# A gated linear recurrence and a squared-ReLU block: first two units by pairs of heads, loads ordered behind x, weights landing in other buffers

## The chip, the cores and the metric

The kernel runs on one core of one Trainium2 chip. The metric is the device time of one execution in microseconds (us). A core has five engines that work at the same time and wait for each other through semaphores: PE (TensorE, matrix products and transposes into PSUM banks), DVE (VectorE, element-wise work), ACT (ScalarE, functions and copies), POOL (GpSimd, here almost only as an issuer of DMAs) and SP (SyncE, an issuer of DMAs). Each engine carries out its own list of instructions strictly in order: one that has to wait holds up all that stand behind it in the list.

## The reference

```python
# (B, H, S, D) = (4, 8, 768, 48); all float32
mag = sqrt(a_re**2 + a_im**2)
scale = minimum(mag, 0.999) / (mag + 1e-06)
a = (a_re + i a_im) * scale                     # a complex gate for each channel
for t in range(S):
    S_re, S_im = a[t] * (S_re + i S_im) + k[t] v[t]^T    # a D x D state per head
    y[t] = q[t] @ S_re
x = y as (3072 tokens, 384)
out = (maximum(x @ w_in, 0) ** 2) @ w_out       # w_in 384 x 2048, w_out 2048 x 384
```

The two weight matrices come in as 64-bit floats and are turned into 32-bit floats on the chip; everything else is 32-bit.

## The kernel before, in words

**Units.** `fast_path` cuts the 3072 tokens into six units of 512. A sequence has 768 tokens, so the second unit (number 1) and the fifth (number 4) hold the end of one sequence and the start of the next ("cross"). Each unit passes through four stages, `load`, `chain`, `pairs` and `dense`; eight heads are held as two halves z = 0, 1 of four heads, and handled as four pairs i = 0..3, two pairs to a half.

**Chain (L822 to L1138), mostly DVE and ACT.** For each half, `roots` (L831: squares, logarithm, exponential, a Newton step) and `normalise` (L852) bring the gates to their scaled form; `inner` (L868) multiplies them up over four neighbouring tokens; `inverse` (L887) forms reciprocals. The totals are transposed on PE (`turned`, L934), run through a scan over the unit (`scan`, L1024, and `scan_x`, L976), and transposed back (L1085). Then `apply` (L1106) makes the scaled queries Q~ and keys K~ of one half: eleven DVE instructions on 128x768 elements (L1117, L1121 four times, L1124, L1126, L1132 four times, keys first), written into the work buffer `ff[z]`. After the two key products `gather` (L1149) copies K~ into the buffer `KC[z]` by DMAs of 32 partitions each, sixteen for each half (twelve where the unit is "cross" or ends a sequence). For units 0 and 1 (`EARLY = 2`) SP issues them, for the others POOL.

**Pairs (L1171).** For each pair of heads Q~ and K~ are transposed into a buffer `QT`: in units 0 and 1 by PE (`turn_pe`, L1202, four steps of four transposes each, ACT copies each out of PSUM), in the others by DVE and twelve DMAs of 64 KB on SP for each pair (`turn`, L1181). Then `score` (L1223) forms the 128x128 products with the mask on DVE, `keep` (L1240) the states K~^T v and their sums, and `mix` (L1271) the output y, which ACT copies to `yts` and SP spreads by two or three DMAs into `xT`, the transposed input of the dense block. `turn_pe` of unit 1 and `keep` take turns on the two PSUM banks `tr0` and `tr1`; `turn_pe` of unit 0 uses the dense banks d0 to d2.

**Dense (L1311), two groups of 256 tokens in a unit.** In a group, eight blocks of two column tiles of W_in (L1326: six products of 128x256 in a block, each shown as two matmuls) go through ReLU and square on ACT (L1333, L1334); then two accumulations over all W_out (L1344), an ACT copy (L1348), and four output DMAs on POOL (L1353).

**Weights.** Each matrix comes in eight pieces of 768 KB (`fetch`, L737, on POOL), and `convert` (L743) makes 32-bit floats of each with one ACT and three DVE instructions (L750, L753, L755, L759). Raw data need a buffer: `raw1` and `raw2` (L713, L719) name it for each piece. Four W_in pieces land in what later holds W_out, three in the g buffers of the dense block, one in the v buffer of unit 1; W_out pieces 0 to 3 take the last two slots of W_out's own buffer in turn, 4, 6 and 7 the three QT buffers, 5 the v buffer of unit 1. A buffer can only be fetched into once what was in it has been used. At the end `inspect` (L761) reads all sixteen pieces once more into the work buffers `ff`, where DVE looks at exponents (L774, L776); `verdict` (L1356) waits for it and for other sums.

**The order.** Nothing is issued as it is written. Every instruction or small group is a step of `Plan` (L481) with an engine, an estimated duration, keys that it reads and writes, and a rank. `order` (L515) runs a list schedule on those estimates: whenever an engine is free it takes the ready step with the lowest rank. The resulting order is emitted, and on the chip each engine keeps to it, with real waits for data and buffers only. So an estimate or a key has two effects: it moves a step in the list of its engine, and it holds nothing at run time. Ranks: pairs (1, n), W_in conversions (2, 0.3), W_out conversions (2, 0.6), chain (2, n), dense and weight fetches (3, ...), inspection (5, i).

Of the kernel before, what the change touches and what calls it, by code (L numbers as in the profile page):

```python
# [576 lines left out]
def fast_path(ctx, tc, q, k, v, a_re, a_im, moe_w_in, moe_w_out, out, flag):  # L577
# [6 lines left out]
    C = 128  # L584
# [53 lines left out]
    xT = sb("xT", NM * 4 * G).rearrange("p (m t) -> p m t", m=NM)  # L638
# [71 lines left out]
    def w2slot(s):  # L710
        return w2u[:, s * 2 * PW:(s + 1) * 2 * PW], [("w2", 2 * s), ("w2", 2 * s + 1)]

    raw1 = ([w2slot(s) for s in (3, 2, 1, 0)]  # L713
# [4 lines left out]
            + [(vv[1].bitcast(U32), [("v", 1)])])  # L718
# [4 lines left out]
            (QT[1].bitcast(U32)[:, 0:2 * PW], [("QT", 1)])]  # L723

# [12 lines left out]
    def fetch(i):  # L737
        src, t, keys, _, n, _ = piece(i)
        dma(pool, [("gate",)], keys,
            lambda: pool.dma_start(out=t.rearrange("p (m f) -> p m f", m=n), in_=src),  # L740
            (CONV, i), 2 * PW * 4 * C, 4.0)

    def convert(i):  # L743
        _, t, keys, dst, n, wk = piece(i)
        t3 = t.rearrange("p (m f two) -> p m f two", m=n, two=2)
# [15 lines left out]
    def inspect(i):  # L761
# [6 lines left out]
        dma(pool, [], keys,  # L768
# [53 lines left out]
    def chain(n):  # L822
# [7 lines left out]

        def roots(z):  # L831
# [3 lines left out]
                accum_out=sums[:, n, z:z + 1]), rank)  # L835
            step("DVE", tt(Y), key(z, 0, 1), key(z, 2), lambda: dve.tensor_tensor(
                out=m2, in0=f0, in1=f1, op=ALU.add), rank)
            step("ACT", ac(Y), key(z, 2), key(z, 0), lambda: act.activation(
                out=f0, in_=m2, func=AF.Ln), rank)
            step("ACT", ac(Y), key(z, 0), key(z, 1), lambda: act.activation(  # L840
                out=f1, in_=f0, func=AF.Exp, scale=-0.5), rank)
            step("ACT", ac(Y), key(z, 1), key(z, 3), lambda: act.activation(
                out=t, in_=f1, func=AF.Square), rank)
# [6 lines left out]
            step("DVE", 2 * tt(Y), key(z, 1, 2, 3), key(z, 3), newton, rank)  # L850

        def normalise(z):  # L852
            f0, f1, _, t = col[z]
            step("ACT", ac(Y), key(z, 3), key(z, 0), lambda: act.activation(
                out=f0, in_=t, func=AF.Copy, scale=0.999), rank)
            step("ACT", ac(Y), key(z, 3), key(z, 1), lambda: act.activation(
                out=f1, in_=t, func=AF.Copy, scale=-1e-6, bias=1.0), rank)
            step("DVE", tt(Y), key(z, 0, 1), key(z, 0), lambda: dve.scalar_tensor_tensor(
                out=f0, in0=f0, scalar=1.0, in1=f1, op0=ALU.min, op1=ALU.mult), rank)
# [3 lines left out]
                op=ALU.mult), rank)  # L863
            step("ACT", ac(Y), key(z, 3), [], lambda: act.activation(
                out=junk[:, 0:Y], in_=t, func=AF.Square, saturate=False,
                accum_out=sums[:, n, 2 + z:3 + z]), rank)
# [133 lines left out]
        def product(dst, xx, y, size, reads, writes):  # L1000
# [16 lines left out]
            step("DVE", 3 * tt(cnt), reads, writes + key(0, 0, 1), go, rank)  # L1017
# [6 lines left out]
        def scan():  # L1024
# [22 lines left out]
            for s in (1, 2, 4):  # L1047
                if s < span:
                    product(tv[:, 0:2, :, s:span], tv[:, 0:2, :, s:span],
                            lambda lo, hi, s=s: tv[:, lo:hi, :, 0:span - s], 40, I, I)  # L1050
                    step("DVE", 0.12, I, I, lambda s=s: minus(top, s, span, tv), rank)
# [54 lines left out]
        def apply(z):  # L1106
            a = A[z].rearrange("p (r h c d) -> p r h c d", r=2, h=HH, c=W)
            qk = QK[z].rearrange("p (r h c d) -> p r h c d", r=2, h=HH, c=W)
            xh = xn.rearrange("p r (h d) -> p r h d", h=H)[:, :, ts(z, HH)]
# [3 lines left out]
            def over(j):  # L1113
                return xh[:, j].unsqueeze(2).to_broadcast([C, HH, W, D])
# [13 lines left out]
            for j in (1, 0):  # L1128
# [6 lines left out]
                if j:  # L1135
                    gather(n, z)
# [322 lines left out]
```

## Time and profile before

| what | us |
|---|---|
| median of three runs (lowest, highest) | 773.3 (770.9, 773.61) |
| the profiled execution | 769.64 |
| its span, first to last instruction | 767.9 |
| PE busy, of the span | 661.5 |
| DVE busy | 506.2 |
| first matmul of the dense block | 106.88 |
| end of the last matmul of the dense block | 756.3 |

The profiled execution took 1.7 us more than its span, and 3.7 us less than the median of the runs. Of a PE row the profile counts two matmuls for each 32-bit product. A "stage" below is a stretch between two times from the start of the span. In the rows of the timeline the first two numbers are start and busy time of a run of equal instructions, and what stands in brackets is the idle time of the engine ahead of it and what ended that. In rows of stages, the numbers behind the stretch are its length, then for each engine the busy time and the number of instructions, then the granted clock of TensorE as a share of full speed (PEclk), the busy share of the DMA engines and their rate.

### The profile page before, as it was taken

How to read it: one execution, taken by the hardware profiler on the slowest of the kernel's cores; microseconds unless marked ns; L12 is line 12 of the kernel's file. 1: busy time of each engine (PE TensorE's matmuls, PEld its weight loads, DVE VectorE, ACT ScalarE, POOL GpSimd, SP SyncE). 2: the span in 40 equal slices, each digit the busy share in tenths (PEclk: the TensorE clock that was granted, in tenths of full speed). 3: DMA queues.
4: the chain of work that ended last, by engine and by line, in shares of the span. 5: the costliest groups of instructions: out<-in, count | busy, mean ns of one | idle time of the engine just before them, and what ended most of it. 6: DMA issues, size and time to landing. Idle time of an engine off the chain costs nothing.

```text
span 767.9 us, 10212 instructions
## 1 busy us (share of the span) xinstructions
PE 661.5 (86%) x3566; PEld 506.5 (66%) x3566; DVE 506.2 (66%) x978; ACT 346.7 (45%) x589; POOL 181.1 (24%) x349
## 2 busy tenths in 40 slices
PE   0014948999998999999999999999999998999994
PEld 0013836777776769858688677588676796686862
DVE  4999987999476797286995287982678975610000
ACT  6762266565466622478322568122765221041320
POOL 5400033420005053051162330250110541311101
PEclk9999977999998999999999999999999999999997
DMA  9721595200713026550046840054600399800000
GB/s 304 229 83 38 151 260 128 42 21 24 194 51 62 2 62 162 149 134 11 11 116 153 170 88 2 23 150 107 185 12 0 83 266 316 292 11 10 11 5 21
DMA packets 55932, 79.43 MB, mean 103 GB/s; under 512 B 11200, under 2 KB 37568, under 8 KB 55872
## 3 DMA queue, kind: packets, MB, share of 16 engines
q1 hardware_dynamic: 40768, 38.95, 19.8%
q0 software_dynamic: 15104, 39.74, 18.5%
q8 instruction: 30, 0.49, 0.3%
q14 instruction: 30, 0.25, 0.1%
HBM read 48.76 MB, written 4.72 MB: 70 GB/s over the span
## 4 chain that ended last, share of the span: by engine, by line
PE 49%; DVE 16%; ACT 7%; DMA 6%; SPq 2%; issue 2%; POOL 0%; DVEq 0%; POOLq 0%; ACTq 0%
PE d L1326 19%; PE d L1344 19%; DMA QT<-aq 5%; PE sc L1233 4%; PE tr L1249 3%; DVE f L876 2%; SPq L1197 2%; DVE f L1012 2%; DVE f L1014 2%; PE yp L1279 2%; DVE e L1016 1%; PE yp L1283 1%; DVE f L1016 1%; PE tr L1216 1%; DVE x L986 1%
## 5 line engine op out<-in xcount | busy, mean ns | idle before, releaser
L1326 PE MATMUL d<-xT,w 128*128 128x256 f32 x1152 | 264.4, 387 | 13.8 <-DMA xT<-yt 13.8
L1344 PE MATMUL d<-w,g 128*128 128x384 f32 x768 | 255.3, 488 | 0.0
L1326 PEld LDWEIGHTS d<-xT,w 128*128 128x128 f32 x1152 | 220.2, 194 | 48.8 <-issue 14.5
L1344 PEld LDWEIGHTS d<-w,g 128*128 128x128 f32 x768 | 144.2, 191 | 94.0 <-issue 2.0
L1353 POOL DMA_DIRECT2D out_dram<-ot x96 | 47.3, 499 | 352.9 <-ACT ot L1348 352.7
L1333 ACT ACTIVATE g<-d 128x512 f32<-128x512 f32 x96 | 57.1, 594 | 127.7 <-PE d L1326 127.6
L818 POOL DMA_DIRECT2D v<-in_v_dram x96 | 55.6, 586 | 91.6 <-PE yp L1283 26.7
L1236 DVE TENSOR_TENSOR A<-sc,mask 128x512 f32<-128x512 f32 x48 | 32.0, 685 | 49.6 <-PE sc L1233 49.6
L1334 ACT ACTIVATE g<-g 128x512 f32<-128x512 f32 x96 | 60.6, 631 | 3.1
L1157 POOL DMA_DIRECT2D KC<-f x104 | 51.0, 497 | 37.0 <-DVE f L1132 18.6
L1233 PE MATMUL sc<-QT 96*128 96x128 f32 x384 | 50.9, 283 | 10.2 <-DMA QT<-aq 7.0
L1233 PEld LDWEIGHTS sc<-QT 96*128 96x128 f32 x384 | 47.6, 196 | 13.9 <-issue 8.2
L1371 DVE TENSOR_SCALAR flag<-tr 1x1 int32<-1x1 f32 x1 | 0.1, 147 | 81.8 <-PE tr L1370 81.8
L1348 ACT COPY ot<-d 128x384 f32<-128x384 f32 x24 | 11.5, 478 | 90.2 <-PE d L1344 80.4
L1121 DVE TENSOR_TENSOR f<-aq,xn 128x768 f32<-128x768 f32 x48 | 42.6, 949 | 1.8 <-ACT xn L1085 1.7
L1132 DVE TENSOR_TENSOR f<-aq 128x768 f32<-128x768 f32 x48 | 43.3, 952 | 0.4
L1289 ACT COPY yt<-yp 112x512 f32<-112x512 f32 x24 | 14.0, 583 | 62.6 <-PE yp L1283 60.4
L1279 PE MATMUL yp<-A,v 128*48 128x128 f32 x384 | 38.0, 283 | 1.6 <-DVE A L1236 1.6
L934 PE MATMUL tr<-perm,xn 128*128 128x128 f32 x36 | 6.1, 301 | 37.3 <-ACT xn L907 37.3
L876 DVE TENSOR_TENSOR f<-aq 128x384 f32<-128x384 f32 x72 | 36.9, 554 | 0.7
L1279 PEld LDWEIGHTS yp<-A,v 128*48 128x48 f32 x384 | 23.1, 125 | 10.6 <-issue 6.3
L934 PEld LDWEIGHTS tr<-perm,xn 128*128 128x128 f32 x36 | 4.7, 153 | 38.6 <-issue 28.8
(145 smaller groups left out, 806.0 us busy)
## 6 DMA issues: line engine op xcount, KB each, us to landing
QT<-aq SPq DMA_DIRECT2D x192, 64.0 KB, 2.4
f<-in_moe_w_in_dram POOLq DMA_DIRECT2D x8, 768.0 KB, 8.7
f<-in_moe_w_out_dram POOLq DMA_DIRECT2D x8, 768.0 KB, 6.9
KC<-f POOLq DMA_DIRECT2D x104, 48.0 KB, 2.1
v<-in_v_dram POOLq DMA_DIRECT2D x96, 48.0 KB, 2.8
out_dram<-ot POOLq DMA_DIRECT2D x96, 48.0 KB, 1.8
xT<-yt SPq DMA_DIRECT2D x36, 96.0 KB, 4.6
aq<-in_a_re_dram SPq DMA_DIRECT2D x8, 384.0 KB, 3.8
```

The source lines that it names most:

```text
L818: lambda i=i, c=c, src=src: pool.dma_start(out=t[32 * c:32 * c + 32, i], in_=src[c]), vrank, 32 * 1536, 4.0,
L876: dve.tensor_tensor(out=f, in0=a[:, :, :, c - 1], in1=a[:, j, :, c].unsqueeze(1).to_broadcast([C, 2, HH, D]), op=ALU.mult)
L1121: lambda j=j, f=f, r=r: dve.tensor_tensor(out=f[:, r], in0=a[:, r], in1=over(j), op=ALU.mult), rank)
L1132: lambda j=j, r=r, o=o: dve.tensor_tensor(out=o[:, :, :, r * D:(r + 1) * D], in0=qk[:, j], in1=a[:, r], op=ALU.mult), rank)
L1157: lambda i=i, c=c: queue.dma_start(out=kc[32 * c:32 * c + 32, i], in_=nat[32 * i:32 * i + 32, c]),
L1233: pe.matmul(sa[:, j], lhsT=T[:, j, 1, h], rhs=T[:, j, 0, h], start=True, stop=True)
L1279: pe.matmul(ypair[64 * h:64 * h + D, ts(j, C)], lhsT=v5[:, j, 2 * i + h], rhs=aa[h][:, j], start=True, stop=at[j] is None)
L1326: pe.matmul(ps[:, j], lhsT=w1[:, f // FP, m, ts(f % FP, C)], rhs=xT[:, m, base:base + G], start=(m == 0), stop=(m == NM - 1))
L1333: act.activation(out=o, in_=ps, func=AF.Relu)
L1334: act.activation(out=o, in_=o, func=AF.Square)
L1344: pe.matmul(ps, lhsT=gt[:, f % 2, ts(i, C)], rhs=w2[:, f], start=(f == 0), stop=(f == NF - 1))
L1353: dma(pool, [("ot", o)], [], lambda c=c, o=o, dst=dst: pool.dma_start(out=dst[c], in_=ots[o][32 * c:32 * c + 32]), rank, 32 * DM * 4)
```

## The change

- **apply by pairs.** In units 0 and 1 `apply` runs once for each pair of heads (`np = 1`): the same eleven instructions on 384 instead of 768 elements, twice; `turn_pe` and `keep` of a pair wait for their own pair only. The copies of K~ go by pairs too (half as long, twice as many), in turn on POOL and SP. Units 2 to 5 keep the whole half and POOL.
- **Loads behind xT.** In the plan, q and k of unit 1, v of every later unit, five W_out pieces (1, 6, 7, then 2, 3) and the inspection depend on an xT being written (that of unit 0, of the unit two before, of unit 0, and of the last unit). W_out pieces 0, 4 and 5 are fetched ahead of the first `pairs`.
- **Buffers.** W_in piece 0 lands in `KC[1]` and piece 7 in the second half of `xT` (which becomes two blocks, one for even units and one for odd) instead of a W_out slot and the v buffer of unit 1.
- **Dense in two parts.** In the first group of each unit the first three blocks begin with the two row tiles m = 0, 1 of xT for their first column tile, and add m = 2 (the last two pairs of heads) afterwards.
- **Ranks and estimates.** `roots` and `normalise` of unit 1 get rank (2, 0.25), ahead of the weight conversions; the scan's products are estimated 0.24 us longer, `minus` at 0.18 for 0.12 us, the xT DMAs with 2.4 for 1.8 us of latency.

```diff
-    xT = sb("xT", NM * 4 * G).rearrange("p (m t) -> p m t", m=NM)
+    xT = sb("xT", 2 * NM * L).rearrange("p (n m t) -> p n m t", n=2, m=NM)
...
-    raw1 = ([w2slot(s) for s in (3, 2, 1, 0)]
+    raw1 = ([(KC[1].bitcast(U32), [("KC", 1, 0), ("KC", 1, 1)])]
+            + [w2slot(s) for s in (2, 1, 0)]
...
-            + [(vv[1].bitcast(U32), [("v", 1)])])
+            )
+    raw1 = [(three(t), keys) for t, keys in raw1]
+    raw1.append((xT[:, 1].bitcast(U32), [("xT", 1, m) for m in range(NM)]))
...
-    def fetch(i):
+    def fetch(i, early=True):
...
-        dma(pool, [("gate",)], keys,
+        dma(pool, [("gate",)] if early else [("xT", 0, NM - 1)], keys,
...
     def inspect(i):
...
-        dma(pool, [], keys,
+        dma(pool, [("xT", (NU - 1) % 2, NM - 1)], keys,
...
     def load(n):
...
-                        dma(queue, [], [(name, z)],
+                        dma(queue, [("xT", 0, NM - 1)] if n == 1 and half else [], [(name, z)],
...
-                dma(pool, [] if n else [("gate",)], [("v", n % 2)],
+                dma(pool, [("xT", n % 2, NM - 1)] if n else [("gate",)], [("v", n % 2)],
...
+        first = (CHAIN, 0.25) if n == 1 else rank
...
-            step("DVE", 3 * tt(cnt), reads, writes + key(0, 0, 1), go, rank)
+            step("DVE", 3 * tt(cnt) + 0.24, reads, writes + key(0, 0, 1), go, rank)
...
-        def apply(z):
+        def apply(z, p, np):
...
+            hs = ts(p, 2) if np == 1 else slice(0, HH)
+            a, qk = a[:, :, hs], qk[:, :, hs]
+            nh = 2 * np
+            n1 = Y * np // 2
...
+            own = ff[z][:, p * Z:(p + np) * Z]
...
-                    gather(n, z)
+                    gather(n, z, p, np)
         for z in range(2):
-            apply(z)
+            if n < EARLY:
+                apply(z, 0, 1)
+                apply(z, 1, 1)
+            else:
+                apply(z, 0, 2)
...
-    def gather(n, z):
+    def gather(n, z, p, np):
...
-                dma(queue, [("f", z, 2), ("f", z, 3)], [("KC", z)],
-                    lambda i=i, c=c: queue.dma_start(
+                queue = sp if n < EARLY and c % 2 else pool
+                dma(queue, keys, [("KC", z, q_) for q_ in range(p, p + np)],
+                    lambda i=i, c=c, queue=queue: queue.dma_start(
...
-                step("PE", 0.46, [("f", z, s4) for s4 in range(4)], [(b,)], go, rank)
+                step("PE", 0.46, [("f", z, 2 * (i % 2) + j) for j in range(2)], [(b,)],
+                     go, rank)
...
     def dense(n, grp):
...
+        split = 3 if grp == 0 else 0
+        for f2, b, ps, o, s in blocks[:split]:
+            f = 2 * f2
+            step("PE", 0.87, [("w1", f // FP)] + [("xT", n % 2, m) for m in range(NM - 1)],
+                 [(b,)], part_of(f, ps[:, 0], range(NM - 1)), rank)
+        for f2, b, ps, o, s in blocks:
             for j in range(2):
                 f = 2 * f2 + j
...
+                late = f2 < split and j == 0
+                step("PE", 0.43 if late else 1.3,
...
+                     part_of(f, ps[:, j], (NM - 1,) if late else range(NM)), rank)
...
             for i in range(NPIECE):
                 fetch(i)
+            for i in range(NPIECE):
+                convert(i)
         chain(n)
         if n == 0:
...
+            for j in (0, 4, 5):
+                fetch(NPIECE + j)
         pairs(n)
         if n == 0:
...
+            for j in (1, 6, 7):
+                fetch(NPIECE + j, False)
+            for j in (0, 1):
+                convert(NPIECE + j)
+            for j in (2, 3):
+                fetch(NPIECE + j, False)
+            for j in range(2, NPIECE):
+                convert(NPIECE + j)
```

More of the change, by code (lines that the diff above doesn't have):

```diff
@@ L723, in fast_path @@
             (QT[1].bitcast(U32)[:, 0:2 * PW], [("QT", 1)])]
+    raw2 = [(two(t), keys) for t, keys in raw2]
     def piece(i):
@@ L849, in newton @@
                                          op0=ALU.add, op1=ALU.mult)
-            step("DVE", 2 * tt(Y), key(z, 1, 2, 3), key(z, 3), newton, rank)
+            step("DVE", 2 * tt(Y), key(z, 1, 2, 3), key(z, 3), newton, first)
         def normalise(z):
@@ L1128, in apply @@
+            for r, op in ((0, ALU.subtract), (1, ALU.add)):
+                step("DVE", tt(n1), kf[0] + kf[1], [("a", z)],
+                     lambda r=r, op=op: dve.tensor_tensor(
+                         out=a[:, r], in0=f4[:, 0, r], in1=f4[:, 1, 1 - r], op=op), rank)
             for j in (1, 0):
-                o = ff[z][:, j * Z:(j + 1) * Z].rearrange("p (c h e) -> p h c e", c=W, h=HH)
+                o = own[:, j * nh * W * R:(j + 1) * nh * W * R].rearrange(
+                    "p (c h e) -> p h c e", c=W, h=nh)
```

120 lines of the change are left out of this document (54 added, 66 removed).

## The prediction

> **What bounds the kernel now.** I read the busy times by stage first, then PE's timeline from the first pair of heads to the second unit's dense block, then DVE's, SP's and POOL's in that stretch, and last PE's waits near the end.
>
> ```profile
> span 767.9 us, 10212 instructions
> 68.00:106.90 38.90, 33.19 (x305) 30.08 (x305) 36.72 (x59) 14.29 (x24) 4.19 (x7) 0.92 0.63 161
> 106.90:119.44 12.54, 2.16 (x6) 1.01 (x5) 9.13 (x12) 11.44 (x16) 6.29 (x12) 0.64 0.97 234
> 119.44:234.00 114.56, 112.90 (x626) 87.58 (x626) 89.99 (x174) 66.55 (x117) 19.78 (x37) 0.98 0.28 72
> 234.00:346.00 112.00, 107.78 (x576) 82.07 (x575) 77.60 (x150) 54.08 (x92) 36.59 (x69) 0.97 0.40 97
> 673.60:756.40 82.80, 82.80 (x323) 60.54 (x321) 0.96 (x4) 21.59 (x37) 7.88 (x16) 1.00 0.04 10
> 756.40:767.90 11.50, 0.05 (x2) 0.00 (x0) 0.15 (x1) 0.45 (x1) 1.96 (x4) 0.63 0.10 26
> ```
>
> From 119.44 on PE hardly rests: 112.90 of 114.56 us, then 107.78 of 112.00, and 82.80 of 82.80 in the last dense block. So the end is the time at which PE gets steady work, plus that work, plus the holes left in it, plus a tail of 11.5 us that the change doesn't touch. The holes are ahead: 10.4 us in 106.90 to 119.44, where the DMA engines are busy at 0.97.
>
> ```profile
> 68.03 5.36 PE L1216 MATMUL d<-ident,f 128*96 128x128 f32 x24 [10.15 <-DVE f L1132]
> 106.88 0.99 PE L1326 MATMUL d<-xT,w 128*128 128x256 f32 x2
> 116.64 1.19 PE L1326 MATMUL d<-xT,w 128*128 128x256 f32 x2 [8.77 <-DMA xT<-yt]
> 119.44 22.62 PE L1326 MATMUL d<-xT,w 128*128 128x256 f32 x92 [1.61 <-DMA xT<-yt]
> 187.12 1.04 PE L1216 MATMUL tr<-ident,f 128*96 128x128 f32 x8
> 195.81 1.14 PE L1249 MATMUL tr<-v,KC 128*96 128x48 f32 x12
> 231.56 0.43 PE L1279 MATMUL yp<-A,v 128*48 128x128 f32 x4
> 237.83 16.68 PE L1326 MATMUL d<-xT,w 128*128 128x256 f32 x62 [3.46 <-DMA xT<-yt]
> ```
>
> Of the rows from 106.88 to 119.44 the first holds the first matmuls of dense unit 0; the next stands 8.77 us until xT lands. But the hinge is the last row: dense unit 1 starts at 237.83, once its own xT is there, and everything behind it is PE work in a row. Between 119.44 and 237.83 PE does dense unit 0 and, from 187.12, pairs of unit 1; pairs start when unit 1's chain is through. An earlier start of dense unit 0 alone therefore buys nothing: PE would run out of it while the pairs of unit 1 go on. **The two bounds on dense unit 1** are PE's own work and unit 1's chain with its pairs. I work out both.
>
> **PE's bound.** The work between is 112.90 us; its cold part is 2.8 us: 92 matmuls took 22.62, 246 ns each, where 66 later take 14.41, 218 ns:
>
> ```profile
> 346.05 14.41 PE L1326 MATMUL d<-xT,w 128*128 128x256 f32 x66
> 66.32 10.15 SPq L1157 DMA_DIRECT2D KC<-f  x16
> 77.71 11.54 SPq L1157 DMA_DIRECT2D KC<-f  x16
> 280.07 6.01 POOL L1157 DMA_DIRECT2D KC<-f  x12 [3.39 <-DVE f L1132]
> KC<-f SPq DMA_DIRECT2D x56, 48.0 KB, 2.0
> xT<-yt SPq DMA_DIRECT2D x36, 96.0 KB, 4.6
> ```
>
> So 110 us after dense unit 0 begins to run freely. When is that? In unit 0 the copies of K~ keep SP from 66.32 to 89.25 (77.71 + 11.54), 0.63 us an issue. With as many on SP (32, of half the size) and as many more on POOL at 0.50 us (6.01 for 12), each batch of eight takes 5 us on SP behind its pair's keys, and the first pair turns about 4 us earlier than 68.03. The last pair's mix ended at 106.9; I estimate 100 (bounds 94, if only K~ held it, and 106.9, if ACT's and PE's lists hold it as before). Then ACT, the issue and the landing: 107 to 119.44 before, 12.5 us under 0.97 of DMA; with q, k, v and five weight pieces behind, about 5, the 4.6 us of the median row. Dense unit 0 starts near 105 (98 to 115; the upper end if POOL's loads still collide), and PE's bound for dense unit 1 is 215 (208 to 225).
>
> **The chain's bound, step by step from 237.83.**
>
> ```profile
> 140.67 1.02 DVE L876 TENSOR_TENSOR f<-aq 128x384 f32<-128x384 f32 x2
> 141.72 0.36 DVE L880 TENSOR_TENSOR aq<-f 128x192 f32<-128x192 f32 x1
> 110.93 0.96 DVE L846 SCALAR_TENSOR_TENSOR f<-f 128x768 f32<-128x768 f32 x1 [2.10 <-ACT f L842]
> 114.06 0.96 DVE L846 SCALAR_TENSOR_TENSOR f<-f 128x768 f32<-128x768 f32 x1 [1.18 <-DMA xT<-yt]
> 126.47 0.56 DVE L753 TENSOR_SCALAR w<-w 128x768 uint32<-128x768 uint32 x1 [3.02 <-DMA w<-in_moe_w_out_dram]
> 129.49 0.96 DVE L759 CUSTOM_DVE_ANT_0 w<-w 128x1536 uint16<-128x1536 uint16 x1 [1.46 <-ACT w L750]
> 176.87 4.43 DVE L1121 TENSOR_TENSOR f<-aq,xn 128x768 f32<-128x768 f32 x5 [0.84 <-ACT xn L1085]
> 183.20 3.57 DVE L1132 TENSOR_TENSOR f<-aq 128x768 f32<-128x768 f32 x4
> 185.19 7.48 SPq L1157 DMA_DIRECT2D KC<-f  x12
> ```
>
> DVE is the pacemaker here: unit 1's `inner` starts at 140.67, behind apply of unit 0 and all conversions, and the four waits above (2.10, 1.18, 3.02, 1.46) are 7.8 us of idle time.
> 1. Halving costs DVE: an instruction of 768 takes 0.89 us in a row (3.57 for 4), two of 384 take 1.05 (141.72 less 140.67), so 0.16 for each of 22 instructions in unit 0: +3.4.
> 2. Weights 0, 4 and 5 of W_out come early, and roots of unit 1 go first, so DVE has work in hand in those waits. Between none and all of 7.8 comes back; I take 5.9, nearer the upper end because the two longest waits are for weights. With step 1: −2.5 (−4.4 to +3.4) at `inner`. The re-ranked steps themselves add nothing, they change places. The early weights run before the first K~ is issued; if they slipped behind it they would cost the forecast one landing of K~, 2.0. W_in piece 0 in K~'s second buffer is converted first of all, long before 77.71, and q and k of unit 1, which leave SP's list ahead of xT, are only used behind `inner`: nothing for these.
> 3. Unit 1's first pair waits for 10 instructions of 0.525, 5.2 us, instead of 176.87 to 186.77, 9.9 (one of z = 1 lay in between): −4.6. The second halves are needed later and lie beside PE's work.
> 4. K~ of unit 1: twelve issues took 7.48 us on SP, so keep followed at 195.81, 8.7 behind the first turn. Six on POOL and six on SP take 3.7, and with 2.0 of landing K~ is there 2.9 sooner. The scores go ahead of keep on PE in any case, so 0 to −2.9; I take −2.2.
> 5. Dense in two parts: three blocks' first parts, 2.6 us of PE work by the plan's three times 0.87, which is the four matmuls of a part at 218 ns, run under the 3.46 us wait: 0 to −2.6; −2.6. In other units no such wait shows, and the split costs nothing, since it only reorders matmuls.
> 6. Four pairs took 44.4 us (187.12 to 231.56), with blocks of dense unit 0 between their steps. If that unit starts near 105, its work ends before the last two pairs, and these don't stand behind blocks: 2 us a pair, −4 (0 to −6).
>
> Sum −15.9: dense unit 1 at 222, 7 us behind PE's bound, so the chain decides and xT's faster landing in unit 0 is more than is needed. Unit 2's chain takes its buffers after unit 1's pairs, so it moves along.
>
> **Behind that.** The inspection's loads share the DMA engines with the last unit's transposes:
>
> ```profile
> 612.14 1.54 POOL L769 DMA_DIRECT2D f<-in_moe_w_in_dram  x2
> 666.08 1.46 POOL L769 DMA_DIRECT2D f<-in_moe_w_out_dram  x2
> QT<-aq SPq DMA_DIRECT2D x192, 64.0 KB, 2.4
> 631.36 6.53 DMA QT<-aq
> 649.84 0.49 PE L1233 MATMUL sc<-QT 96*128 96x128 f32 x2 [1.04 <-DMA QT<-aq]
> 653.01 1.91 PE L1233 MATMUL sc<-QT 96*128 96x128 f32 x10 [2.68 <-DMA QT<-aq]
> 486.20 0.55 PE L934 MATMUL tr<-ident,f 128*128 128x128 f32 x3 [1.33 <-ACT f L1080]
> ```
>
> A transpose's DMA takes 6.53 against a median of 2.4, and PE waits 1.04 + 2.68 = 3.7 us. Behind the last xT the inspection no longer meets them: −3.7. Its cover is the last dense block, 82.8 us, and it took 55 (612.14 to 667.54); DVE is idle there, so it costs nothing unless it takes over 80. The wait of 1.33 at L934 comes of a scan estimated too short; longer estimates put other products first: −1.0 (0 to −1.3). v behind xT moves little, its buffer was bound to the same pairs.
>
> All: 769.64 − 15.9 − 3.7 − 1.0 = 749.0 for a profiled execution. The median of the runs lies 3.7 higher (773.3), so **752.7**.
>
> **The rivals.**
> - PE's bound holds, since the pairs go faster than I think: dense unit 1 at 212, 10 earlier than the forecast's 222: **742.7**. For it: dense unit 0 would be used up by 200 and nothing else holds PE. Against it: the pairs share two banks, four turns and a keep each, one behind the other.
> - The cold stretches go as well.
>
> ```profile
> 122.00:124.00 2.00, 2.00 (x6) 1.55 (x6) 1.46 (x1) 0.74 (x2) 0.51 (x1) 0.50 0.83 134
> ```
>
> PE runs at 0.50 after the idle stretch ahead of dense unit 0. Dense unit 1 begins slowly as well: 16.68 − 62 x 0.218 = 3.2 us too long. If PE is kept busy up to both starts, the 2.8 of the first lies in slack and 3.2 is gained: **749.5**. The Trainium skill's page "TensorE: Matmul & The Clock Gate", section "What's actually happening", says that an idle window of some 3.4 us halves the clock and a busy one restores it; the trace agrees (0.50 at 122, behind holes of 8.77 and 1.61). By it this rival needs holes below that, while my forecast leaves 7 us of holes, and so I give the 3.2 no credit.
> - The gain is hidden: PE's and ACT's lists for unit 1's pairs keep their pace (step 6 nothing, step 4 nothing), step 2 gives nothing back (+3.4): dense unit 1 at 237.83 + 3.4 − 4.6 − 2.6 = 234, and only half of the later holes' 4.7 goes: **767.1**.
> - The other side: late weights. In the list of POOL the 32 DMAs of v for units 1 and 2 go ahead of the W_out pieces that wait for a slot.
>
> ```profile
> 116.29 4.80 POOL L818 DMA_DIRECT2D v<-in_v_dram  x8 [0.25 <-issue]
> 121.80 5.90 DMA QT<-in_moe_w_out_dram
> ```
>
> Before, the last piece was issued behind such v's and landed at 127.7. DVE's list has the conversions ahead of `inner`, so it stands. From about 154 on (two conversions, 5 us, `inner` at 159, 18 after 140.67) the loss equals the gains of steps 3 to 6 (13.4) and of the later holes (4.7). Two pieces landing one after the other at 165 would give 773.3 + 11 = **784**. Against it: eight v's take 4.8 us, 32 about 20, from 105 to 125.
> - It does not do what it says: the hold on q, k and v is one of order, no engine waits for xT. POOL's list could reach its loads while xT is still on the way. Then dense unit 0 starts at 115, PE's bound is 225: **755.7**.
>
> **How the numbers follow.** Forecast 0.43, PE's bound 0.17, cold stretches 0.07, hidden 0.20, late weights 0.09, collision 0.04. About 0.5% (3.9 us) is what a measurement of this kernel can tell from no change. Faster by more: all of the first three, the collision, and 0.12 of hidden: 0.83. Within: 0.08 of hidden, 0.02 of late weights: 0.10. Slower: 0.07. The range reaches from PE's bound at its early end (208, 14 before the forecast's 222, that is 738.5 in round numbers) to the hidden case plus 2.4 (769.5); late weights and the outer tails of both ends, some 0.18, are left out.
>
> **What would show it.** First turn of unit 0 near 64; K~ in eights on both queues; xT of unit 0 landing within 5 us; dense unit 0 from about 105; `inner` of unit 1 near 138; its first turn near 180; dense unit 1 near 222 with holes on PE ahead of it; no long waits for QT in the last unit; the inspection done before the last dense block. I am wrong if dense unit 1 starts after 234 or the later holes grow.

## The result, and the profile after

The changed kernel takes 748.4 us (median of four runs, 744.9 to 751.56) against 773.2 for the kernel before: ratio 0.968 [0.964, 0.973]. The forecast was 752.7 in a range of 738.5 to 769.5. Its profiled execution took 747.83 us, with a span of 746.1.

First the stages of the changed kernel, cut at the same events as those shown of the kernel before (first turn of unit 0, first matmul of dense unit 0, its free run up to PE's last work before dense unit 1, and the tail); the columns are those explained there.

```profile
63.20:95.86 32.66, 30.16 (x304) 27.35 (x304) 31.29 (x65) 16.37 (x28) 16.91 (x35) 1.00 0.46 111
95.86:100.81 4.95, 3.01 (x14) 2.14 (x13) 4.85 (x6) 2.16 (x3) 4.95 (x10) 1.00 0.82 194
100.81:219.91 119.10, 114.03 (x626) 87.21 (x626) 106.14 (x216) 72.44 (x124) 36.78 (x68) 0.97 0.38 103
730.90:746.10 15.20, 0.03 (x2) 0.00 (x0) 0.15 (x1) 0.43 (x1) 1.96 (x4) 0.65 0.08 19
```

Unit 0's pairs take 32.7 us where they took 38.9, and the stretch in which xT had to land shrank from 12.5 to 5.0 us. In the long stretch behind it DVE now works 106 of 119 us (90 of 115 before): PE is no busier than it was, DVE is. The tail grew from 11.5 to 15.2.

PE's timeline of the changed kernel, at the same places as before (L1239 turns, L1273 keeps, L1342 W_in products, L1382 W_out products):

```profile
63.20 3.50 PE L1239 MATMUL d<-ident,f 128*96 128x128 f32 x16 [5.36 <-DVE f L1150]
67.37 2.05 PE L1257 MATMUL sc<-QT 96*128 96x128 f32 x16 [0.67 <-ACT QT L1243]
100.81 18.37 PE L1342 MATMUL d<-xT,w 128*128 128x256 f32 x84 [1.94 <-issue]
132.27 5.49 PE L1382 MATMUL d<-w,g 128*128 128x384 f32 x8 [3.76 <-DVE w L769]
178.57 1.04 PE L1239 MATMUL tr<-ident,f 128*96 128x128 f32 x8
182.91 1.14 PE L1273 MATMUL tr<-v,KC 128*96 128x48 f32 x12
191.88 1.14 PE L1273 MATMUL tr<-v,KC 128*96 128x48 f32 x12
202.19 1.14 PE L1273 MATMUL tr<-v,KC 128*96 128x48 f32 x12
211.16 1.14 PE L1273 MATMUL tr<-v,KC 128*96 128x48 f32 x12
223.56 13.51 PE L1342 MATMUL d<-xT,w 128*128 128x256 f32 x54 [3.65 <-DMA xT<-yt]
635.61 1.35 PE L1257 MATMUL sc<-QT 96*128 96x128 f32 x10 [0.50 <-DMA QT<-aq]
```

Dense unit 0 runs freely from 100.81 (119.44 before), at full pace (84 in 18.37, 219 ns each). It stops twice for W_out pieces that DVE is still converting, for 1.31 and 3.76 us; these two waits are all of PE's idle time between 100.81 and 219.91. Dense unit 1 starts at 223.56 (237.83), again behind a wait for its xT, and the last unit waits 0.50 for QT where it waited 3.72.

On DVE of the changed kernel, `inner` (L888) starts before the W_out conversions (L769) are through, and unit 1's apply (L1134) starts at 167.75:

```profile
117.06 1.02 DVE L888 TENSOR_TENSOR f<-aq 128x384 f32<-128x384 f32 x2
143.77 0.96 DVE L769 CUSTOM_DVE_ANT_0 w<-QT,w 128x1536 uint16<-128x1536 uint16 x1
167.75 1.02 DVE L1134 TENSOR_TENSOR aq<-aq,xn 128x384 f32<-128x384 f32 x2
172.03 1.97 DVE L1139 TENSOR_TENSOR f<-aq,xn 128x384 f32<-128x384 f32 x4 [3.26 <-ACT xn L1097]
192.51 1.97 DVE L1150 TENSOR_TENSOR f<-aq 128x384 f32<-128x384 f32 x4
```

From 55.7 to that apply DVE stood idle for 2.0 us in all; before, for 10.6 up to 174.21. Behind it stands a new wait of 3.26 for ACT (0.84 before), and apply ends at 194.5. In the kernel before, the last rows of apply on DVE and the fourth keep on PE are:

```profile
191.26 3.56 DVE L1132 TENSOR_TENSOR f<-aq 128x768 f32<-128x768 f32 x4
226.05 1.14 PE L1249 MATMUL tr<-v,KC 128*96 128x48 f32 x12
```

The time between events, from the timelines of PE, DVE and ACT; the last column is a second profile of the changed kernel (the run called e12 below, whose profiled execution took longest of its six):

| stretch | before | changed | changed, again |
|---|---|---|---|
| start to unit 1's apply on DVE | 174.21 | 167.75 | 171.36 |
| to the first turn of unit 1 | 12.91 | 10.82 | 10.10 |
| to its first keep | 8.69 | 4.34 | 4.33 |
| to its fourth keep | 30.24 | 28.25 | 28.51 |
| to dense unit 1's free run | 11.78 | 12.40 | 13.00 |
| to the last copy on ACT | 518.54 | 507.29 | 508.19 |
| tail | 11.53 | 15.25 | 15.31 |
| span | 767.9 | 746.1 | 750.8 |

Two profiles of the same kernel differ by 3.6 us at unit 1's apply. Where a single profile is compared below, differences under about 4 us carry no verdict; the medians do.

### The profile page after: what moved, and what is told of

It reads as the page before. It is cut to its first block, busy times and chain, and to the rows that moved or that the text cites. A ratio compares the mean times of both kernels' runs of the same rounds, so it can differ in the third digit from the quotient of the medians.

```text
span 746.1 us, 10395 instructions
## 1 busy us (share of the span) xinstructions
PE 655.4 (88%) x3566; PEld 502.6 (67%) x3566; DVE 510.8 (68%) x1022; ACT 347.0 (47%) x589; POOL 209.9 (28%) x405
## 4 chain that ended last, share of the span: by engine, by line
PE 66%; DVE 14%; SPq 8%; DMA 4%; issue 2%; ACT 2%; POOL 0%; DVEq 0%; POOLq 0%; ACTq 0%
PE d L1382 28%; PE d L1342 27%; SPq L1221 5%; PE sc L1257 3%; DVE f L888 3%; PE tr L1273 2%; PE yp L1303 2%; PE tr L946 1%; PE yp L1307 1%; SPq L1320 1%; DMA QT<-aq 1%; SPq L814 1%; DMA xT<-yt 1%; DMA aq<-in_k_dram 1%; DVE aq L873 1%
## 5 line engine op out<-in xcount | busy, mean ns | idle before, releaser
L1382 PE MATMUL d<-w,g 128*128 128x384 f32 x768 | 261.8, 494 | 5.1 <-DVE w L769 5.1
L1342 PE MATMUL d<-xT,w 128*128 128x256 f32 x1152 | 256.4, 381 | 5.6 <-DMA xT<-yt 3.6
L1342 PEld LDWEIGHTS d<-xT,w 128*128 128x128 f32 x1152 | 218.4, 191 | 39.1 <-issue 7.2
L1382 PEld LDWEIGHTS d<-w,g 128*128 128x128 f32 x768 | 143.9, 192 | 98.0 <-DVE w L769 6.1
L1181 POOL DMA_DIRECT2D KC<-f x160 | 78.4, 498 | 103.4 <-DVE f L1150 48.6
L1370 ACT ACTIVATE g<-d 128x512 f32<-128x512 f32 x96 | 57.0, 593 | 107.0 <-PE d L1342 106.7
L1371 ACT ACTIVATE g<-g 128x512 f32<-128x512 f32 x96 | 60.6, 631 | 3.1
L1139 DVE TENSOR_TENSOR f<-aq,xn 128x384 f32<-128x384 f32 (+1 forms) x64 | 44.2, 747 | 11.9 <-ACT xn L1097 11.9
L1150 DVE TENSOR_TENSOR f<-aq 128x384 f32<-128x384 f32 (+1 forms) x64 | 44.8, 751 | 0.5
L888 DVE TENSOR_TENSOR f<-aq 128x384 f32<-128x384 f32 x72 | 36.9, 553 | 0.8
L1303 PE MATMUL yp<-A,v 128*48 128x128 f32 x384 | 36.2, 277 | 0.2
L1273 PEld LDWEIGHTS tr<-v,KC 128*96 128x96 f32 x320 | 29.5, 165 | 2.3 <-issue 1.3
L1273 PE MATMUL tr<-v,KC 128*96 128x48 f32 x320 | 29.7, 246 | 0.3 <-DMA KC<-f 0.2
```

Of the source, the lines that this page charges most:

```text
L888: dve.tensor_tensor(out=f, in0=a[:, :, :, c - 1], in1=a[:, j, :, c].unsqueeze(1).to_broadcast([C, 2, HH, D]), op=ALU.mult)
L1150: lambda j=j, r=r, o=o: dve.tensor_tensor(out=o[:, :, :, r * D:(r + 1) * D], in0=qk[:, j], in1=a[:, r], op=ALU.mult), rank)
L1181: lambda i=i, c=c, queue=queue: queue.dma_start(out=kc[32 * c:32 * c + 32, i], in_=nat[32 * i:32 * i + 32, c]),
L1273: pe.matmul(ps[:, j, h], lhsT=kc[:, j, (2 * i + h) % HH], rhs=v5[:, j, 2 * i + h], start=True, stop=True)
L1303: pe.matmul(ypair[64 * h:64 * h + D, ts(j, C)], lhsT=v5[:, j, 2 * i + h], rhs=aa[h][:, j], start=True, stop=at[j] is None)
L1342: pe.matmul(ps, lhsT=w1[:, f // FP, m, ts(f % FP, C)], rhs=xT[:, n % 2, m, ts(grp, G)], start=(m == 0), stop=(m == NM - 1))
```

## Experiments

The changed kernel's own median was 748.4 us at first and 750.0 when it ran again beside e9 to e11. Differences to it below are to the first; by the second, what a kernel takes more is 1.6 smaller, and what it takes less 1.6 larger. Ratios are to the kernel before, run beside it.

**Is it DVE's chain or PE that sets dense unit 1?** Three kernels leave work out: one on DVE, one on PE, one both.

```diff
 # e1_dve_less, in convert(i): the last step of a W_out conversion is left out
+        if i >= NPIECE:
+            return
         step("DVE", tt(PW), keys + [("lo", i)], wk,
```

> Leaves out the last of the three DVE instructions of each W_out conversion (the low bits of the weight), 8 x 0.96 = 7.7 us of DVE work ahead of unit 1's scan; the plan knows it. Chain theory (DVE's work up to unit 1's pairs sets the start of dense unit 1): the first turn of unit 1 comes 6 to 8 us before 178.6, dense unit 1 runs on from about 216 to 218 instead of 223.56, and the run is 5 to 7 us faster than the changed kernel. PE theory (PE's own work behind the start of dense unit 0 sets it): the first turn comes earlier but dense unit 1 stays within 2 us of 223.56, and the time within 2 us.

Measured: 740.8 us, 0.960 [0.954, 0.965], 7.6 below the changed kernel (9.2 by its second median) for 7.7 us of DVE work. PE's timeline of this kernel:

```profile
166.33 1.04 PE L1241 MATMUL tr<-ident,f 128*96 128x128 f32 x8
...
212.96 4.48 PE L1344 MATMUL d<-xT,w 128*128 128x256 f32 x20
```

In this profile (of its lowest time, 737.1) the first turn comes 12 us earlier, and dense unit 1 starts at 212.96 without any wait for xT: in this one execution PE's own work has become the bound, at the place where the forecast had put it (212 to 215).

```diff
 # e2_pe_less, in dense: row tile m = 1 left out in the second group of dense unit 0
+        less = n == 0 and grp == 1
...
-                     part_of(f, ps[:, j], (NM - 1,) if late else range(NM)), rank)
+                     part_of(f, ps[:, j], (NM - 1,) if late else (0, 2) if less else range(NM)), rank)
```

> Leaves out one of the three row tiles in the W_in products of dense unit 0's second group, 32 matmuls of 0.215 = 6.9 us of PE work between dense unit 0 and dense unit 1; the plan knows it. Chain theory: PE gets holes instead, dense unit 1 stays within 2 us of 223.56, time within 2 us of the changed kernel. PE theory: dense unit 1 from about 217, 5 to 7 us faster.

Measured: 746.1, 0.966 [0.960, 0.971]: 2.3 below the changed kernel (3.9 by its second median) for 6.9 us of PE work, and the intervals overlap. Where the work went, in PE's timeline of this kernel:

```profile
222.81 13.45 PE L1342 MATMUL d<-xT,w 128*128 128x256 f32 x54 [6.64 <-DMA xT<-yt]
```

The wait for xT grew from 3.65 to 6.64 and dense unit 1 moved by 0.75 only. Dense unit 0 began 3.4 later in this profile (104.17), which takes up about the rest of the 6.9: less PE work turns into a longer wait.

> Both of these left out. Chain theory: the same as with DVE's part alone, dense unit 1 at 216 to 218. PE theory: the same as with PE's part alone, about 217. If the two bounds lie within some us of each other, each alone gives only a part and both together give about 7 us.

With both edits: 740.6, 0.958 [0.953, 0.964], level with the DVE edit alone. Its wait for xT is back (3.85, dense unit 1 at 217.11). What PE lost could not be used, since the chain decides again. The chain's bound is shown: DVE work pays about one for one, PE work pays 2 to 4 of 6.9 us alone and nothing beside DVE's.

**What do the pairs of heads bring?**

```diff
 # e4_whole_halves, in chain; turn_pe and keep wait for the whole half again,
 # K~ still goes over both queues
-            if n < EARLY:
-                apply(z, 0, 1)
-                apply(z, 1, 1)
-            else:
-                apply(z, 0, 2)
+            apply(z, 0, 2)
...
```

> Only the pairs are undone: apply takes whole halves in units 0 and 1 again, with whole-half copies of K~ (still on two queues); all else as changed. My steps: DVE 3.4 us less in unit 0, first turn of unit 0 at about 67.5, first turn of unit 1 4.6 us later less that 3.4, K~ of unit 1 up to 2.9 later: dense unit 1 at 224 to 228, so 1 to 5 us slower than the changed kernel. Rival (the pairs carry the gain, because they bring unit 0's last products and with them dense unit 0 forward): dense unit 0 7 us later and the run 7 us or more slower.

Measured: 744.6, 0.964 [0.958, 0.969]. Undoing the title part of the change costs nothing; if anything it gains 3.8. The expectation missed. It was taken up again in e10 to e12.

**What do the loads bring?** All buffers, holds and fetch orders as before but for the inspection's, the rest as changed (the diff is the load and buffer part of the change, backwards).

> Undoes the loads and buffers alone: W_in piece 0 in a W_out slot and piece 7 in unit 1's v buffer again, W_out fetched in the old order, nothing of q, k, v and weights ordered behind xT; pairs of heads, split, ranks, estimates and the inspection's place stay. Load theory (now the first, as undoing the pairs cost nothing): xT of unit 0 lands late again and DVE waits for weights again, dense unit 0 runs freely from 112 to 119, first turn of unit 1 3 to 6 us later, dense unit 1 at 230 to 237, 7 to 13 us slower than the changed kernel. Rival (the order of unit 1's roots and the estimates made the gain): within 3 us of the changed kernel.

Measured: 753.7, 0.978 [0.975, 0.981], 5.3 above the changed kernel. PE's timeline of this kernel:

```profile
111.72 20.00 PE L1341 MATMUL d<-xT,w 128*128 128x256 f32 x84 [8.48 <-DMA xT<-yt]
231.47 14.69 PE L1341 MATMUL d<-xT,w 128*128 128x256 f32 x60 [3.29 <-DMA xT<-yt]
```

The old wait for unit 0's xT is back (8.48), and DVE's longest wait in the stretch is 3.86 us for ACT. Dense unit 0 starts 11 us later, dense unit 1 eight. The loads are worth some 5 us, less than the 7 to 13 expected.

**What does the new rank of unit 1's roots bring?** One line.

```diff
-        first = (CHAIN, 0.25) if n == 1 else rank
+        first = rank
```

> Undoes one line: roots and normalise of unit 1 get their old rank, behind the weight conversions. DVE's work is the same, only its order differs. Load theory: first turn of unit 1 within 2 us of 178.6, W_out earlier on PE, dense unit 1 within 2 us of 223.56. Rival (the order carries the gain): first turn 5 us or more later, dense unit 1 at 229 or later, 5 us slower.

Measured: 758.0, 0.982 [0.979, 0.985]: 9.6 above the changed kernel. The expectation that little would change fell. DVE's timeline of this kernel:

```profile
115.35 0.96 DVE L858 SCALAR_TENSOR_TENSOR f<-f 128x768 f32<-128x768 f32 x1 [4.56 <-ACT f L854]
120.55 0.96 DVE L858 SCALAR_TENSOR_TENSOR f<-f 128x768 f32<-128x768 f32 x1 [3.24 <-ACT f L854]
```

Before the first of them stands the addition (L848) that the logarithm of each half needs, and much later come two more waits, those of the reciprocals (L911):

```profile
108.98 1.82 DVE L848 TENSOR_TENSOR f<-f 128x768 f32<-128x768 f32 x2
158.25 0.96 DVE L911 SCALAR_TENSOR_TENSOR f<-f 128x768 f32<-128x768 f32 x1 [1.78 <-ACT f L907]
164.85 0.96 DVE L911 SCALAR_TENSOR_TENSOR f<-f 128x768 f32<-128x768 f32 x1 [2.79 <-ACT f L907]
```

ACT's timeline has, ahead of DVE's first wait:

```profile
109.43 0.60 ACT L1370 ACTIVATE g<-d 128x512 f32<-128x512 f32 x1 [6.86 <-PE d L1342]
...
110.59 0.83 ACT L850 ACTIVATE f<-f 128x768 f32<-128x768 f32 x1
111.45 0.60 ACT L1370 ACTIVATE g<-d 128x512 f32<-128x512 f32 x1
...
114.49 0.82 ACT L854 ACTIVATE f<-f 128x768 f32<-128x768 f32 x1
```

With the old rank the first half's addition stands on DVE behind conversions and runs at 108.98, where the changed kernel has it at 83.83. ACT's logarithm, exponential and square of unit 1 (L850, L852, L854) then fall among the ReLU and square of dense unit 0's first blocks (L1370, L1371), which lie ahead of the logarithm and between each two of the three. In the changed kernel the first half's three ran from 84.81 to 87.75 and the second half's from 101.95 to 104.54, ahead of all ReLU. The 6.86 us for which ACT waits ahead of the first ReLU cost little by themselves: DVE's first addition ends only near 109.9 (half of its row), and the logarithm starts at 110.59. What costs is the mixing: DVE waits 4.56 and 3.24 for L854. And since `inner` now stands behind the last conversion (145.42, not 117.06), no conversion is left to fill the waits at the reciprocals, 1.78 and 2.79 where the changed kernel has one of 0.75. So the rank pays on both lists: unit 1's functions come ahead of dense unit 0's on ACT, and its steps on DVE lie between conversions. The two were not tried apart.

**Dense in two parts.**

```diff
-        split = 3 if grp == 0 else 0
+        split = 0
```

> Undoes the dense block in two parts alone. By my step 5 the eight matmuls that ran under the wait for unit 1's xT (1.7 us) stand behind it: 1 to 3 us slower, the wait ahead of dense unit 1 at 5 to 6 us instead of 3.65, other units unchanged. Rival (the first parts only take the place of other products in PE's list): within 1 us.

Measured: 749.3, 0.972 [0.968, 0.976], 0.9 above the changed kernel and inside its interval. The wait for xT is 5.40 instead of 3.65, and dense unit 1 starts at 224.05. So the split shortens the wait by 1.75 us, of the 2.6 that it can cover. Right in direction, too small for a verdict.

**The inspection behind the last xT.**

```diff
-        dma(pool, [("xT", (NU - 1) % 2, NM - 1)], keys,
+        dma(pool, [], keys,
```

> Undoes one line: the inspection's loads are not ordered behind the last xT. By my reckoning PE waits 2.7 to 3.7 us more for QT in the last unit (0.50 us now) and the run is 3 to 4 us slower. Rival (the waits in the kernel before were of its order and not of the inspection): no wait above 1.5 us in the last unit, within 1 us.

Measured: 765.6 (759.02 to 767.51), 0.991 [0.988, 0.995]. That is 17 above the changed kernel by the medians, 11 by the two spans: far more than the 3 to 4 expected. Dense unit 1 starts at 224.57, so it is all behind that. PE's timeline near the end:

```profile
631.89 1.35 PE L1257 MATMUL sc<-QT 96*128 96x128 f32 x10 [1.29 <-DMA QT<-aq]
649.73 2.47 PE L1257 MATMUL sc<-QT 96*128 96x128 f32 x10 [4.58 <-DMA QT<-aq]
661.55 18.37 PE L1342 MATMUL d<-xT,w 128*128 128x256 f32 x84 [2.32 <-DMA xT<-yt]
```

8.2 us of waits and 1.1 of slow scores (10 in 2.47 instead of 1.35) where the changed kernel has 0.5. 1.4 us of the profile's 11 are not placed, nor the 6.6 by which the median is further off than this profile, the lowest of its five times.

**Would the two cheap edits alone have done it?** e9 is the kernel before with the new rank and the inspection's hold, and nothing else.

> The kernel before with two edits alone: roots and normalise of unit 1 ahead of the weight conversions, and the inspection behind the last xT. Undone in the changed kernel, each of the two cost some 10 us. Theory A, each edit pays by itself: DVE's idle time up to unit 1's apply falls from 10.6 us by the 3.3 of the two waits for ACT and xT at L846 but not by the two waits for weights (3.0 and 1.5), so apply and the first turn of unit 1 come 3 to 4 us earlier, dense unit 1 starts near 234, and the 3.7 us of QT waits in the last unit go: 764 to 767. Theory B, the two carry most of the change, as their undoing says: 752 to 757, dense unit 1 before 228. Theory C, the order pays only with the other loads, since without them the conversions have no weights to work on: dense unit 1 within 1.5 us of 237.8, only the inspection's 3.7 gained: 768 to 771.

Measured: 767.6 (765.12 to 770.61), where the kernel before took 772.1 beside it: 0.994 [0.992, 0.996]. Of some 10 and 11 to 17 us that the undoing of each costs, 4.4 in all come when they are made alone. Theory B is out; the time lies at the edge between A and C. DVE waits in another place: its timeline has

```profile
130.43 0.96 DVE L759 CUSTOM_DVE_ANT_0 w<-w 128x1536 uint16<-128x1536 uint16 x1 [4.83 <-ACT w L750]
```

and its idle time up to apply falls only from 10.6 to 9.0. This wait is for ACT's part of a conversion (L750, at 129.50), which stands in ACT's list behind ReLU steps that wait for PE. That the early weights of the changed kernel would have filled it is argued; no run has the rank and the loads without the rest. The inspection's hold failed for another reason, seen on POOL's queue of this kernel:

```profile
613.56 5.85 POOL L1159 DMA_DIRECT2D KC<-f  x12 [4.69 <-PE tr L1251]
619.40 2.44 POOL L769 DMA_DIRECT2D f<-in_moe_w_in_dram  x3
```

and on that of the changed kernel:

```profile
608.24 5.87 POOL L1181 DMA_DIRECT2D KC<-f  x12 [6.62 <-PE tr L1273]
633.95 1.96 POOL L1391 DMA_DIRECT2D out_dram<-ot  x4 [19.84 <-ACT ot L1386]
635.90 3.08 POOL L779 DMA_DIRECT2D f<-in_moe_w_in_dram  x4
```

The hold is one of order. In the changed kernel the loads stand behind an output DMA that waits 19.84 us for ACT, and start at 635.90; in e9 they stand right behind K~ and start at 619.40, among the last transposes, and the last unit waits 1.80, 2.48 and 0.73 for QT. What holds them is the instruction in front, not xT: even in the changed kernel they start 7 us before SP issues the last DMA into xT (642.7).

**Pairs in unit 1 only, whole halves, and the changed kernel, side by side.**

```diff
 # e10_unit1_pairs; turn_pe of unit 0 waits for the whole half
-            if n < EARLY:
+            if n == 1:
...
```

> The changed kernel with whole halves in unit 0 and pairs of heads in unit 1 only. If the pairs cost only DVE's 3.4 us in unit 0 and pay 4.6 at unit 1's first turn, this version has both: unit 1's apply near 166, first turn near 176, dense unit 1 near 220.5, 742 to 745 and below the run with whole halves in both units. If the first turn isn't what decides (whole halves in both units ended dense unit 1's wait at the same 223 with a first turn as late), it is level with that run: within 1.5 us of it.

> Whole halves in both units, once more, beside the changed kernel itself in the same call. If halving costs what DVE's 22 instructions more than it saves, this is 3 to 5 us below the changed kernel, as the two medians of different calls had it (744.6 and 748.4). If the pairs are worth nothing either way, the two lie within 2 us.

> The changed kernel itself, as the yardstick for the three other kernels of this call: 745 to 751, its first turn of unit 1 near 178.6 and dense unit 1 near 223.6.

| run side by side | median (range) us | ratio to the kernel before |
|---|---|---|
| e12, the changed kernel | 750.0 (748.11 to 752.49) | 0.971 [0.968, 0.974] |
| e10, pairs in unit 1 only | 748.0 (746.75 to 748.16) | 0.968 [0.965, 0.971] |
| e11, whole halves | 746.0 (744.6 to 746.62) | 0.966 [0.963, 0.969] |

The changed kernel and the one with whole halves do not overlap: 4.1 us in favour of whole halves, as in the first comparison (3.8). Pairs in unit 1 cost half of it (2.0, e10 against e11), pairs in unit 0 the other half. The expectation of e10 missed on both sides: it is neither below e11 nor within 1.5 us of it. Of the kernels that compute all of the output, whole halves take the least: 0.964 (e4) and 0.966 of the kernel before. PE's timeline of e10 shows where the pairs' gain goes (turns L1243, keeps L1277):

```profile
176.91 1.04 PE L1243 MATMUL tr<-ident,f 128*96 128x128 f32 x8
190.21 1.14 PE L1277 MATMUL tr<-v,KC 128*96 128x48 f32 x12
202.26 1.14 PE L1277 MATMUL tr<-v,KC 128*96 128x48 f32 x12
211.98 1.14 PE L1277 MATMUL tr<-v,KC 128*96 128x48 f32 x12
```

and that of e11 (turns L1235, keeps L1269):

```profile
180.39 1.04 PE L1235 MATMUL tr<-ident,f 128*96 128x128 f32 x8
184.72 1.14 PE L1269 MATMUL tr<-v,KC 128*96 128x48 f32 x12
193.87 1.14 PE L1269 MATMUL tr<-v,KC 128*96 128x48 f32 x12
202.85 1.14 PE L1269 MATMUL tr<-v,KC 128*96 128x48 f32 x12
211.82 1.14 PE L1269 MATMUL tr<-v,KC 128*96 128x48 f32 x12
```

By pairs the first turn is 3.5 us earlier, in the direction of step 3 and below its 4.6. Then the third keep comes 12.05 behind the second, where whole halves keep to 9.0, and at the fourth keep e10 is 0.2 behind. PE waits for nothing that its timeline shows between these rows; its list is another one. Ahead of the third keep e10 has 2.75 us of W_out products where e11 has 1.46, and the scores (1.8 from start to start) stand before that keep and not behind it: 3.1 us, all of the loss. The third and fourth pairs belong to the second half, whose apply DVE ends at 191.85 in e10 and at 188.74 in e11. That the plan puts the third keep back because of that later end is argued, not shown; what is shown is that 22 halved instructions finish later, and that the earlier first turn is gone at the fourth keep.

## Why the prediction was right, step by step

The sum was right (749.0 for a profiled execution, 747.8 measured; dense unit 1 at 222, 223.6 measured), and so was the bound: the chain decides, with PE's bound 8.7 us ahead of it (100.81 + 114.03 = 214.8; forecast 215). e1 to e3 show it. The forecast left out that PE waits for W_out pieces on its way, 5.1 us in all; with them PE had no hole from 132.27 to 219.91, so only 3.65 of the 8.7 were to be had without faster conversions. The terms under the sum moved about more than the sum did, and that they met in it is in part luck: dense unit 1 came 1.6 us later than forecast, the work behind it 6.6 shorter, the tail 3.7 longer, together 1.3 less. In the second profile dense unit 1 came at 227.3 and the time was 752.5.

- **PE's bound.** First turn 63.20 (forecast 64), dense unit 0 from 100.81 (105), xT landing in 2.6 us by the median instead of 4.6: as forecast, and slack, as forecast. In the second profile the free run began at 105.05. The cold part of dense unit 0's first run before is 2.6 and not the 2.8 of the prediction (22.62 − 92 x 0.218); it lies in the slack too.
- **Steps 1 and 2**, forecast −2.5: unit 1's apply came 6.5 earlier, and 2.9 in the second profile. DVE got back 8.6 of its 10.6 us of waits, in the second profile 5.5. Here one sentence failed outright: "The re-ranked steps themselves add nothing, they change places." Undoing the rank costs 9.6 us (e6). I looked at DVE's work alone; the steps also changed places on ACT, ahead of dense unit 0's ReLU and squares, and on DVE they now share the stretch with conversions. `inner`, forecast near 138, started at 117.06, between conversions, which I had kept ahead of it. The price of halving was too high: 0.16 for each instruction, read from two of 384 with the hand-over to the next step in it (and 22 x 0.16 is 3.5, not 3.4). In a row four of 384 take 1.97 and four of 768 take 3.56, so 0.09 for each and 2.1 a unit.
- **Step 3**, forecast −4.6: apply to first turn shrank by 2.1, since DVE now waits 3.26 for ACT in it, and what the first turn gains is lost by the third pair (e10). The reason that failed is "The second halves are needed later and lie beside PE's work": DVE finished apply at 194.5, against 194.8 before (191.26 + 3.56), though it began 6.5 earlier, and from the third pair on the order on PE gave the gain back. Together with step 1 the pairs cost about 4 us instead of gaining 1.2 (e4, e11).
- **Step 4**, forecast −2.2, bound −2.9: keep followed the first turn by 4.34 instead of 8.69, so 4.35. It isn't due to the pairs: with whole halves on two queues it is 4.33 as well (e11), nor to the loads (4.33 in e5). With one queue and the old estimates it is 7.40 (e9). The two queues and the new estimates were undone in no run by themselves, so which of them brings it is open. The forecast had kept the scores ahead of keep; the new list puts the first keep before them (182.91 and 183.88).
- **Step 6**, forecast −4: first to fourth keep took 28.25 instead of 30.24. Steps 4 and 6 make 6.3 together, against 6.2. Whole halves need 27.1 (e11), so this gain isn't the pairs' either.
- **Step 5**, forecast −2.6: twelve matmuls ran ahead of the wait instead of four, worth 1.7 at 218 ns; the forecast had counted all twelve as new. e7 could not tell it from nothing.
- **Behind dense unit 1**, forecast −4.7: −11.3. Waits from 238 on fell from some 10.7 to 4.5 (those for ACT at the transposes behind the scan went altogether, 2.65 where I took 1.0; that the longer estimates did it was not tried by itself), the slow stretch at the start of dense unit 1 from 3.2 to 1.7 (13.51 − 54 x 0.218), the split's 1.7 is in it too; some 2 us are not placed. The last unit gained 3.2 of the 3.7. The inspection ended at 690, inside the last dense block and not before it, with 40 us to spare.
- **The tail**, "a tail of 11.5 us that the change doesn't touch": it grew by 3.7 (below), which takes back over half of what the last point gave beyond its forecast.

Of the rivals, late weights did not come (last conversion 143.77, after `inner`, not ahead of it), the gain was not hidden, and the slow stretch at dense unit 1 stayed, behind a wait of 3.65, at a granted clock of 0.50 until about 226.8. That agrees with the rule of the Trainium skill that the prediction names. The rival that the hold is one of order only was true in its mechanism (e9), and harmless for the inspection because an output DMA happens to stand in front. For v of unit 1 the key does not even name an xT: what was last written there when the plan reads it is W_in piece 7, in the same half of the buffer.

## What to carry to other kernels

Where one engine's in-order list is the pacemaker, ask of every moved step what stands in front of it on all the engines that it uses: here one of the largest parts, 8 to 10 us, was one rank. It brought three ACT functions ahead of another block's ReLU and squares, and it left DVE conversions to fill later waits with. Cutting instructions in two to start a consumer earlier makes the engine that does them finish later; compare the end of the block, not its beginning. The parts did not add: two edits that cost 10 and over 11 us when undone gave 4.4 together when made alone, so price a part both ways before calling it the cause.

## What the runs showed of the hardware

**The same scores at two speeds.** In the second profile of the changed kernel (e12) PE's timeline begins so:

```profile
63.26 3.65 PE L1239 MATMUL d<-ident,f 128*96 128x128 f32 x16 [5.36 <-DVE f L1150]
67.58 3.78 PE L1257 MATMUL sc<-QT 96*128 96x128 f32 x16 [0.67 <-ACT QT L1243]
227.30 14.22 PE L1342 MATMUL d<-xT,w 128*128 128x256 f32 x54 [4.25 <-DMA xT<-yt]
```

Sixteen matmuls of the first scores took 3.78 us where the first profile has 2.05, behind the same waits of 5.36 and 0.67. Of the nine profiles with pairs of heads in unit 0, five show 2.05 and four 3.78 (e2, e3, e6, e12); the five with whole halves in unit 0, where 24 matmuls of transposes go ahead in a row, show 1.95 to 2.39. The first turn, which sets in after the long wait, runs at 204 to 228 ns a matmul in all nine (3.27 to 3.65 for sixteen), where the second turn of the first profile takes 120 (1.92). The granted clock of e12 reads 1.00 in this stretch all the same:

```profile
67.50:71.50 4.00, 3.92 (x19) 3.92 (x20) 1.90 (x5) 0.03 (x1) 3.01 (x7) 1.00 0.28 69
```

So the record does not show a gated clock here. The Trainium skill's page "TensorE: Matmul & The Clock Gate", section "What's actually happening", says that the gate's window of some 3.4 us runs freely, so that the point at which a busy PE gets its clock back varies from run to run. The 3.27 to 3.65 us of transposes ahead of the scores lie just at that length, which would explain the two speeds; the clock record of these runs does not bear it out, and it was not tried by itself. In e12 unit 1's apply comes 3.6 later than in the first profile; DVE's idle time up to it is 3.1 longer (5.1, not 2.0), nearly all in waits for scores of unit 0. So the slow scores may be part of what pairs in unit 0 cost.

**The pace after a wait.** Dense unit 1's first run took 220 ns a matmul behind a wait of 2.55 us (e4: 60 in 13.19), but 247 behind 2.62 (e11: 60 in 14.83), 250 behind 3.65 and 263 behind 4.25. Here the clock record agrees: it reads 1.00 all through e4's start, and 0.50 in e11 from 224.5 to about 227.8. The waits of e4 and e11 are too near to each other for a threshold between them, and lie below the 3.4 us of that page of the Trainium skill: a full pace is not assured below it.

**A longer end.** From the last copy on ACT to the end of the span the kernel before takes 11.5 us and e9 11.7, all kernels with the rest of the change 14.2 to 15.5: 14.2 to 14.6 with whole halves in unit 0 (e4, e10, e11), 15.0 to 15.5 with pairs there. So some 0.9 us of what pairs cost lies here (14.4 in e11, 15.3 in e12). After the last four output DMAs (2.6 to 3.6 us to landing in the changed kernel) no instruction of any engine stands there. What it is stays open; no run took it apart.
